# A causal mask in four GpSimd instructions, one per head, in place of one: a memory-augmented attention layer on one Trainium2 core

## The chip, the cores and the metric

The kernel runs on one core of one Trainium2 chip. The metric is the device time of one execution in microseconds (us); smaller is better. Three runs of the kernel before took 332.82, 332.64 and 334.40 us, so its median is 332.82 us.

The core has five engines with queues of their own. In the profile they are PE (TensorE, matrix products; PEld are its weight loads), DVE (VectorE), ACT (ScalarE), POOL (GpSimd) and SP (SyncE, which here only issues DMA transfers). Each works through its own queue in order and waits on semaphores for the others.

## The reference

The input is a sequence of 2048 rows of 640 values in bfloat16. It is normalised, and then goes two ways that are multiplied at the end: a recurrent attention with 32 heads of width 20, and a gated linear unit. The attention goes through the rows in 4 segments of 512. Within a segment each head does causal softmax attention; beside it each head reads a memory that the earlier segments have filled.

```
xn = layernorm(x)
per segment s (512 rows), per head (Dh = 20):
    logits = q k^T * Dh**-0.5 + mask          # mask: key after query -> -1e9
    a_dot  = softmax(logits) v
    a_mem  = (phi(q) M) / (phi(q) z + 1e-6)   # phi(t) = t + 1 if t > 0 else exp(t)
    o      = sigmoid(beta) * a_mem + (1 - sigmoid(beta)) * a_dot
    M += phi(k)^T v ;  z += sum phi(k)
s   = o @ wo
g   = silu( (sigmoid(xn @ w_gate) * (xn @ w_up)) @ w_down )
out = x + s * g
```

## The kernel before

**Tiles.** Rows lie in tiles of 128. The 32 heads are taken in 8 groups of four, and the groups in 4 pairs per segment. The scores of a pair are worked out transposed (keys on the partitions, queries along the free axis), and only the blocks on and below the diagonal. They come in five batches, called units u = 0 to 4 (table `UNITS`, lines 42 to 48). A unit fills one PSUM tile `Sps` of 128 x 4 heads x 512; there is only one such tile, and the function `scores` (line 555) fills it with products of 24 rows, for the four heads side by side on the array. ScalarE then takes the exponential of the whole tile into an SBUF tile `pt` (line 566, four buffers). Units 0 and 3 hold four blocks of the diagonal for each head (unit 0 those of the pair's first group, unit 3 those of its second), and in these the half that the causal mask forbids is set to zero by GpSimd, in place in `pt` (line 569). There are 4 segments x 4 pairs x 5 = 80 units and 32 masks.

**Who uses a masked tile.** `weigh_group` (line 603) multiplies the `pt` tiles of a group with the values into the PSUM tile `AT`, 28 products for four heads, four side by side, with the head as the inner loop; the blocks of unit 0 come first in a first group's products, those of unit 3 last in a second group's, behind 12 others. For the first group of a pair that is at the start of unit 3, three units after its mask; for the second group at the start of the next pair, two units after its mask. ScalarE copies the result to `ats` (line 615), a DMA transposes it (`Asb`, line 618), and VectorE divides by the row sums in `divide`: `rd` (lines 595 and 596) and `od` (line 598). For the last pair `weigh` (line 576) does the same without the detour (`Aps`).

**The rest of the work.** Projections (`v_tile`, `k_chunk`, `q_chunk`), the gated unit (`gate`, `up`, `down`; `hT` at line 484 is its hidden layer on VectorE), the memory (`m_update`, `mem_read`; `om` at line 457), the output projection (`o_proj`, `aa` and `xr` at lines 543 and 549) and the layer norm of the next segment (`ln_stats`, `ln_norm`; `xn` at line 292, transposed by DMA into `xnT`, line 302 or 304) are laid between the units.

**What sets the order.** The program is written out completely by Python. Each unit is a slot; a list of due times by segment (`PLAN`) and the estimated TensorE costs of the tasks say into which slot each task goes. So the order of the instructions in every queue is fixed, and durations on the chip do not change it. On VectorE a late instruction holds up all behind it. The GpSimd queue holds, between the masks: the two steps of `rstd` (lines 280 and 281) that `xn` needs, the additions of `om` to `od` (line 512), those of the memory (line 439), and at the end three of the last additions (line 549). Before the first mask it fills constants with memsets and makes two 0/1 patterns with short affine selects (lines 219 to 251). SP issues all DMAs but the late weights.

Of the kernel before, what the change touches and what calls it, by code (L numbers as in the profile page):

```python
# [9 lines left out]
P = 128  # L10
# [20 lines left out]
ALU = mybir.AluOpType  # L31
# [67 lines left out]
def kernel(  # L99
# [14 lines left out]
    nc = tc.nc  # L114
# [93 lines left out]
    def load_late(name, src, a, b):  # L208
        parts = src.shape[0] // P
        if a == 0:  # L210
# [9 lines left out]
                            base=0, pattern=[[-1, P]], channel_multiplier=1)  # L220
# [86 lines left out]
    def half_tile(tiles, n, half):  # L307
        return tiles[(2 * n + half) % 3]
# [246 lines left out]
    def scores(n, pair, u):  # L555
        half = pair // 2
        qt, kt = half_tile(QT, n, half), half_tile(KT, n, half)
        for (dg, kb, qb, cnt, c0) in UNITS[u]:
            gi = 2 * pair % 4 + dg
            for r in range(4):  # L560
                nc.tensor.matmul(Sps[:, r, c0:c0 + cnt * P],  # L561
                                 lhsT=kt[32 * r:32 * r + KR, gi, kb * P:(kb + 1) * P],
                                 rhs=qt[32 * r:32 * r + KR, gi, qb * P:(qb + cnt) * P],
                                 start=True, stop=True, tile_position=(32 * r, 0))
        pt = ptp.tile([P, 4, L], BF, name="pt")
        nc.scalar.activation(pt[:], Sps[:], ACT.Exp, scale=SCALE)  # L566
        if u in (0, 3):
            diag = pt[:].rearrange("p r (x c) -> p (r x) c", c=P)
            nc.gpsimd.affine_select(out=diag, in_=diag, compare_op=ALU.is_ge, fill=0.0, base=0,  # L569
                                    pattern=[[0, 16], [1, P]], channel_multiplier=-1)  # L570
        return pt

    def parts(dg):
# [193 lines left out]
    for n in range(NSEG):  # L767
# [46 lines left out]
        for slot in range(NSLOT):  # L814
            pair, u = divmod(slot, NU)
            now = NSLOT * n + slot
            share = max(level - fixed[slot], 0.0)
            if u == 0 and (n or pair):
                q = n * (NG // 2) + pair - 1
                weigh_group(now, q // (NG // 2), q % (NG // 2), 1, pts)  # L820
                pts = {}
            elif u == 3 and not old(n, pair):
                weigh_group(now, n, pair, 0, pts)
            pts[u] = scores(n, pair, u)
            delay[0] = True
            goal += FIRST * share
            fill(now + 0.45, (tasks,))
            flush()
            for w in due:
                weigh(*w)  # L830
            delay[0] = False
            while first and first[0][0] < now + 1.0:
                run_task(first)
            due = []
            if old(n, pair) and u in (2, 4):
                due.append((n, pair, u // 4, pts))
            goal += (1.0 - FIRST) * share
            fill(now + 1.0, (tasks, soft))
            split()
# [46 lines left out]
```

## Time and profile before

The profile holds one further execution, of 334.05 us, with a span from first to last instruction of 332.2 us.

| what | value |
|---|---|
| median of three runs | 332.82 us |
| the profiled execution | 334.05 us |
| its span | 332.2 us |
| TensorE clock granted, mean | 0.998 |
| PE busy | 319.7 us |
| DVE busy | 235.4 us |
| ACT busy | 241.6 us |
| POOL busy | 115.6 us, of which 64.5 us are the 32 masks |

In a row of a timeline stand the start in us from the span's start, the duration in us, engine, source line, operation, what is written and read, shapes and count; rows that follow one another on an engine and are alike are merged (x2). A bracket at the end gives the idle time of the engine ahead of it and what ended it. In a row of the waits view stand who waited for whom, the sum in us, how many times, and the longest. Idle time on PE is counted between modelled ends.

### The profile page before, as it was taken

The numbers are of one execution on the slowest core, as the hardware profiler recorded it, in microseconds if no ns is written. First come the engines' busy times: TensorE is split into PE (matmuls) and PEld (weight loads), VectorE is DVE, ScalarE is ACT, GpSimd is POOL, SyncE is SP. The second block draws the span as 40 slices with busy tenths as digits, with TensorE's granted clock in tenths as the row PEclk, the third lists the DMA queues.
The fourth block names the chain that finished last, engine by engine and source line by source line (L and its number), as shares of the span: only waits on it lengthen the run. The fifth ranks groups of instructions, "written<-read, shape, count | busy, mean of one in ns | idle before, by whom it ended". The sixth has DMA issues, their size and how long they took to land.

```text
span 332.2 us, 8456 instructions
## 1 busy us (share of the span) xinstructions
PE 319.7 (96%) x3426; PEld 172.9 (52%) x3426; DVE 235.4 (71%) x516; ACT 241.6 (73%) x271; POOL 115.6 (35%) x137
## 2 busy tenths in 40 slices
PE   8999979999899999999999999999999999899994
PEld 7544445444464564554466455554456555444673
DVE  6276746699779769679976977767666769746545
ACT  3653879898898675686887877776897888688720
POOL 6636222222217022273314522353414232443304
PEclk9999999999999999999999999999999999999999
DMA  7965993598931650444651286134520252320032
GB/s 217 343 215 182 196 210 94 148 217 211 263 106 24 115 128 25 126 126 69 174 137 43 55 136 100 54 108 123 148 78 16 46 128 58 95 77 18 3 63 81
DMA packets 71111, 39.49 MB, mean 119 GB/s; under 512 B 44960, under 2 KB 71072, under 8 KB 71072
## 3 DMA queue, kind: packets, MB, share of 16 engines
q1 hardware_dynamic: 68800, 36.17, 45.1%
q10 hardware_dynamic: 2272, 2.79, 3.1%
q8 instruction: 27, 0.44, 0.5%
q14 instruction: 12, 0.10, 0.1%
HBM read 20.19 MB, written 8.39 MB: 86 GB/s over the span
## 4 chain that ended last, share of the span: by engine, by line
PE 75%; DVE 13%; DMA 7%; issue 3%; ACT 1%; POOL 0%; SPq 0%; DVEq 0%; ACTq 0%
PE yp L499 14%; PE gp L467 13%; PE up L479 12%; PE Sps L561 6%; PE psk L328 6%; PE sp L541 6%; PE AT L611 5%; PE psq L360 5%; PE psv L399 4%; DMA xnT<-xn 4%; DMA Cs<-cb 1%; DVE q L362 1%; PE dm L427 1%; DVE hT L484 1%; DVE rd L596 1%
## 5 line engine op out<-in xcount | busy, mean ns | idle before, releaser
L566 ACT ACTIVATE pt<-Sps 128x2048 bf16<-128x2048 f32 x80 | 150.4, 1880 | 25.4 <-PE Sps L561 25.2
L569 POOL TENSOR_SCALAR_AFFINE_SELECT pt<-pt 128x2048 bf16<-128x2048 bf16 x32 | 64.5, 2017 | 175.3 <-ACT pt L566 175.3
L479 PE MATMUL up<-xnT,Wu 128*128 128x512 bf16 x240 | 63.2, 380 | 0.7 <-DVE aa L543 0.5
L467 PE MATMUL gp<-xnT,Wg 128*128 128x512 bf16 x240 | 62.5, 380 | 0.0
L499 PE MATMUL yp<-Wd,hT 128*128 128x320 bf16 x384 | 56.9, 300 | 1.0 <-DVE hT L484 1.0
L484 DVE SCALAR_TENSOR_TENSOR hT<-tg,up 128x512 bf16<-128x512 bf16 x48 | 32.7, 682 | 18.7 <-PE up L479 13.5
L499 PEld LDWEIGHTS <-hT 128*128 128x128 bf16 x384 | 35.6, 98 | 19.0 <-issue 3.6
L471 ACT ACTIVATE tg<-gp 128x512 bf16<-128x512 f32 x48 | 28.7, 598 | 9.2 <-PE gp L467 9.1
L479 PEld LDWEIGHTS <-Wu 128*128 128x128 bf16 x240 | 21.5, 98 | 25.9 <-issue 4.0
L467 PEld LDWEIGHTS <-Wg 128*128 128x128 bf16 x240 | 21.6, 98 | 24.3 <-issue 2.1
L561 PE MATMUL Sps<-QT,KT 24*128 24x128 bf16 (+2 forms) x896 | 32.5, 241 | 0.8 <-DMA QT<-Cs 0.4
L505 DVE SCALAR_TENSOR_TENSOR aa<-t,yp 128x320 bf16<-128x320 bf16 x32 | 15.3, 481 | 19.3 <-ACT t L503 19.1
L399 PE MATMUL psv<-Wv,xnT 128*128 128x320 bf16 x160 | 25.7, 299 | 2.3 <-DMA xnT<-xn 2.2
L615 ACT CAST ats<-AT 128x512 bf16<-128x512 f32 x30 | 17.6, 586 | 14.0 <-PE AT L611 13.5
L541 PE MATMUL sp<-Wo,oT 128*128 128x320 bf16 x160 | 25.6, 299 | 0.6 <-DVE om L457 0.6
L561 PEld LDWEIGHTS <-KT 24*128 24x128 bf16 x896 | 13.4, 92 | 23.1 <-issue 21.2
L360 PE MATMUL psq<-xnT,Wq 128*128 128x512 bf16 x100 | 23.6, 379 | 0.5 <-DVE q L362 0.5
L328 PE MATMUL psk<-xnT,Wk 128*128 128x512 bf16 x100 | 24.0, 379 | 0.0
L611 PE MATMUL AT<-pt,va 128*32 128x128 bf16 (+1 forms) x840 | 22.1, 244 | 0.8 <-DVE om L457 0.8
L543 DVE SCALAR_TENSOR_TENSOR aa<-aa,sp 128x320 bf16<-128x320 bf16 x32 | 15.4, 483 | 9.1 <-PE sp L541 8.9
L611 PEld LDWEIGHTS <-va 128*32 128x32 bf16 x840 | 14.5, 97 | 13.7 <-issue 6.4
L598 DVE TENSOR_TENSOR od<-Asb,rd 128x320 bf16<-128x320 bf16 x30 | 20.8, 694 | 1.0
(81 smaller groups left out, 374.8 us busy)
## 6 DMA issues: line engine op xcount, KB each, us to landing
KT<-Ks SPq DMA_DIRECT2D x32, 80.0 KB
QT<-Qs SPq DMA_DIRECT2D x32, 80.0 KB
xr<-in_A_x_dram SPq DMA_DIRECT2D x15, 160.0 KB
out_dram<-xr SPq DMA_DIRECT2D x15, 160.0 KB
xt<-in_A_x_dram SPq DMA_DIRECT2D x6, 320.0 KB
Wg<-in_B_w_gate_dram SPq DMA_DIRECT2D x3, 640.0 KB
Wu<-in_B_w_up_dram SPq DMA_DIRECT2D x3, 640.0 KB
Wd<-in_B_w_down_dram ACTq DMA_DIRECT2D x4, 480.0 KB
```

Source lines behind the costliest of these rows:

```text
L328: nc.tensor.matmul(ps[:], lhsT=W["k"][:, k, c * P:(c + 1) * P], rhs=s["xnT"][:, k, :], start=(k == 0), stop=(k == DC - 1))
L360: nc.tensor.matmul(ps[:], lhsT=W["q"][:, k, c * P:(c + 1) * P], rhs=s["xnT"][:, k, :], start=(k == 0), stop=(k == DC - 1))
L399: nc.tensor.matmul(ps[:], lhsT=s["xnT"][:, k, j * P:(j + 1) * P], rhs=W["v"][:, k, half * HB:(half + 1) * HB], start=(k == 0), stop=(k == ...
L467: nc.tensor.matmul(gp[:], lhsT=Wg[f // 4][:, k, fo:fo + P], rhs=s["xnT"][:, k, :], start=(k == 0), stop=(k == DC - 1))
L479: nc.tensor.matmul(ps[:], lhsT=Wu[f // 4][:, k, fo:fo + P], rhs=s["xnT"][:, k, :], start=(k == 0), stop=(k == DC - 1))
L484: empty(lambda: nc.vector.scalar_tensor_tensor(out=h[:], in0=tg[:], scalar=1.0, in1=ps[:], op0=ALU.add, op1=ALU.mult), own)
L499: nc.tensor.matmul(yp[:], lhsT=s["hT"][f][:, j * P:(j + 1) * P], rhs=W["d"][:, f, hs], start=(f == 0), stop=(f == FC - 1))
L541: nc.tensor.matmul(sp[:], lhsT=s["oT"][:, j, c, :], rhs=W["o"][:, c, hs], start=(c == 0), stop=(c == DC - 1))
L561: nc.tensor.matmul(Sps[:, r, c0:c0 + cnt * P], lhsT=kt[32 * r:32 * r + KR, gi, kb * P:(kb + 1) * P], rhs=qt[32 * r:32 * r + KR, gi, qb * P ...
L566: nc.scalar.activation(pt[:], Sps[:], ACT.Exp, scale=SCALE)
L569: nc.gpsimd.affine_select(out=diag, in_=diag, compare_op=ALU.is_ge, fill=0.0, base=0, pattern=[[0, 16], [1, P]], channel_multiplier=-1)
L611: nc.tensor.matmul(AT[32 * r:32 * r + 32, qb * P:(qb + cnt) * P], lhsT=v[:, h0:h0 + 32], rhs=pts[u][:, r, c0:c0 + cnt * P], start=(i == 0) ...
```

## The change

In `scores`, the mask of units 0 and 3 is no longer one affine select over the whole tile (128 partitions x 2048 elements, 16 blocks of 128) but a loop over the four heads. Each of the four instructions handles 128 partitions x 512 elements (4 blocks of 128), in place, with the same condition. Number and place of the calls of `scores` stay as they are; so do all other instructions and their order. In all there are 128 selects in place of 32.

```diff
         nc.scalar.activation(pt[:], Sps[:], ACT.Exp, scale=SCALE)
         if u in (0, 3):
-            diag = pt[:].rearrange("p r (x c) -> p (r x) c", c=P)
-            nc.gpsimd.affine_select(out=diag, in_=diag, compare_op=ALU.is_ge, fill=0.0, base=0,
-                                    pattern=[[0, 16], [1, P]], channel_multiplier=-1)
+            for r in range(4):
+                diag = pt[:, r, :].rearrange("p (x c) -> p x c", c=P)
+                nc.gpsimd.affine_select(out=diag, in_=diag, compare_op=ALU.is_ge, fill=0.0, base=0,
+                                        pattern=[[0, 4], [1, P]], channel_multiplier=-1)
         return pt
```

## The prediction

> **What bounds the kernel now.** I read the page first, then the waits of PE, then the timelines of POOL and DVE side by side. The page:
>
> ```profile
> span 332.2 us, 8456 instructions
> PE 319.7 (96%) x3426; PEld 172.9 (52%) x3426; DVE 235.4 (71%) x516; ACT 241.6 (73%) x271; POOL 115.6 (35%) x137
> ...
> PE 75%; DVE 13%; DMA 7%; issue 3%; ACT 1%; POOL 0%; SPq 0%; DVEq 0%; ACTq 0%
> ...
> L569 POOL TENSOR_SCALAR_AFFINE_SELECT pt<-pt 128x2048 bf16<-128x2048 bf16 x32 | 64.5, 2017 | 175.3 <-ACT pt L566 175.3
> ```
>
> PE is the bound. POOL idles two thirds of the span, a mask takes 2.02 us, and POOL is not on the chain of waits at all. But DVE holds 13% of that chain, some 43 us. So the question is what holds DVE up, and how much of that reaches PE. From the view of the waits, PE's rows that end in DVE, or in a DMA behind DVE:
>
> ```profile
> PE psv L399 <- DMA xnT<-xn: 2.2, 2, 1.8
> PE yp L499 <- DVE hT L484: 1.0, 1, 1.0
> PE AT L611 <- DVE om L457: 0.8, 2, 0.5
> PE sp L541 <- DVE om L457: 0.6, 1, 0.6
> PE up L479 <- DVE aa L543: 0.5, 1, 0.5
> PE psq L360 <- DVE q L362: 0.5, 1, 0.5
> ```
>
> The last five rows sum to 3.4 us, in six waits. The timelines at those places, masks on POOL first, then DVE:
>
> ```profile
> 36.44 2.01 POOL L569 TENSOR_SCALAR_AFFINE_SELECT pt<-pt 128x2048 bf16<-128x2048 bf16 x1 [5.76 <-ACT pt L566]
> ...
> 80.93 2.00 POOL L569 TENSOR_SCALAR_AFFINE_SELECT pt<-pt 128x2048 bf16<-128x2048 bf16 x1 [7.53 <-ACT pt L566]
> ...
> 98.65 2.00 POOL L569 TENSOR_SCALAR_AFFINE_SELECT pt<-pt 128x2048 bf16<-128x2048 bf16 x1 [8.31 <-ACT pt L566]
> ...
> 124.67 2.00 POOL L569 TENSOR_SCALAR_AFFINE_SELECT pt<-pt 128x2048 bf16<-128x2048 bf16 x1 [6.61 <-ACT pt L566]
> ...
> 155.96 2.00 POOL L569 TENSOR_SCALAR_AFFINE_SELECT pt<-pt 128x2048 bf16<-128x2048 bf16 x1 [5.77 <-ACT pt L566]
> ...
> 270.86 2.00 POOL L569 TENSOR_SCALAR_AFFINE_SELECT pt<-pt 128x2048 bf16<-128x2048 bf16 x1 [3.97 <-ACT pt L566]
> ...
> 280.09 2.00 POOL L569 TENSOR_SCALAR_AFFINE_SELECT pt<-pt 128x2048 bf16<-128x2048 bf16 x1 [7.23 <-ACT pt L566]
> ...
> 286.61 2.20 POOL L569 TENSOR_SCALAR_AFFINE_SELECT pt<-pt 128x2048 bf16<-128x2048 bf16 x1 [4.51 <-ACT pt L566]
> 288.78 2.52 POOL L512 TENSOR_TENSOR od<-od,om 128x320 bf16<-128x320 bf16 x3
> ```
>
> ```profile
> 36.36 2.62 DVE L292 TENSOR_SCALAR xn<-xt,mv,rstd 128x640 bf16<-128x640 bf16 x2
> ...
> 81.09 2.19 DVE L598 TENSOR_TENSOR od<-Asb,rd 128x320 bf16<-128x320 bf16 x1
> ...
> 124.93 1.77 DVE L596 TENSOR_TENSOR rd<-rd,omg 128x16 f32<-128x16 f32 x1
> 126.73 0.49 DVE L598 TENSOR_TENSOR od<-Asb,rd 128x320 bf16<-128x320 bf16 x1
> ...
> 156.06 2.25 DVE L598 TENSOR_TENSOR od<-Asb,rd 128x320 bf16<-128x320 bf16 x1
> ...
> 271.91 0.98 DVE L596 TENSOR_TENSOR rd<-rd,omg 128x16 f32<-128x16 f32 x1
> ...
> 280.62 1.82 DVE L549 TENSOR_TENSOR xr<-aa,xr 128x640 bf16<-128x640 bf16 x1
> ...
> 287.15 1.69 DVE L596 TENSOR_TENSOR rd<-rd,omg 128x16 f32<-128x16 f32 x1
> 288.87 1.04 DVE L598 TENSOR_TENSOR od<-Asb,rd 128x320 bf16<-128x320 bf16 x1
> ```
>
> Here is the finding. The same `od` takes 0.49 us at 126.73 and 2.19 us at 81.09. The long one ends at 83.28, 0.35 after the mask that began just ahead of it (80.93 + 2.00 = 82.93); the one at 156.06 ends at 158.31, again 0.35 after its mask. `rd` at 124.93 ends at 126.70 and at 287.15 at 288.84, each 0.03 after its mask's end; `xr` at 280.62 ends 0.35 after. All these read SBUF alone. So such an instruction, caught by a mask, stands until the mask is through, up to 2 us, and DVE's queue stands behind it. Each of PE's six waits above comes behind one of these.
>
> **The change part by part.** First the length of the pieces, and what happens between two of them:
>
> ```profile
> 1.10 0.29 POOL L219 TENSOR_SCALAR_AFFINE_SELECT ident<-ident 128x128 bf16<-128x128 bf16 x1
> ...
> 24.79 0.39 POOL L250 TENSOR_SCALAR_AFFINE_SELECT BD<-BD 128x168 bf16<-128x168 bf16 x1
> 25.13 0.47 POOL L248 TENSOR_SCALAR_AFFINE_SELECT BD<-BD 128x168 bf16<-128x168 bf16 x1
> ```
>
> ```profile
> 24.38 0.97 DVE L292 TENSOR_SCALAR xn<-xt,mv,rstd 128x640 bf16<-128x640 bf16 x2
> ```
>
> Selects of 128 and of 2048 elements take 0.29 and 2.00 us: 0.89 ns an element and 0.18 us fixed, so 0.18 + 512 x 0.89 ns = 0.63 us for a head (bounds: a quarter of 2.00, 0.50, and the 0.39 us of 168 elements plus 344 x 0.89 ns, 0.70). The select at 25.13 begins 0.05 before the end of the one at 24.79 (25.18), whose data it doesn't touch. So four heads take 4 x 0.63 - 3 x 0.05 = 2.37 us, 0.37 more than now (from 4 x 0.50 - 0.15 = 1.85, 0.15 less, to 4 x 0.70 + 3 x 0.07 = 3.0, 1.0 more, with the gap of 0.07 that the dependent select at 24.79 has behind 24.21 + 0.51). Times 32 that is 12 us of POOL, which idles 65%: nothing by itself.
>
> Who waits for the longer mask? PE, at the `AT` products. Where the mask ends nearest to them:
>
> ```profile
> 61.81 0.40 PE L561 MATMUL Sps<-QT,KT 24*128 24x128 bf16 x16
> ...
> 68.84 0.40 PE L561 MATMUL Sps<-QT,KT 24*128 24x128 bf16 x16
> ...
> 101.08 0.81 PE L611 MATMUL AT<-pt,va 128*32 128x256 bf16 x28
> ```
>
> The mask at 98.65 ends at 100.65; the group begins at 101.08, and its masked blocks are the last 16 of 28. So there is at least 0.43 us of cover at the tightest place, and 0.37 fits. On PE itself each head's products now want their own mask: 3 x 32 more waits. At 68.84 the four heads' operands have just come by four separate DMAs, so four waits stand in those 16 products; at 61.81 none do. Both take 0.40 us. I take nothing for a wait already met. The adds and `rstd` behind a mask on POOL come 0.37 us later, at worst once each on the path: I allow 0.4 us in all.
>
> Now the gain. A caught DVE instruction need only wait for the end of one head, if it is let in there. It was at the boundary at 25.18: the second `xn` (the pair ends at 25.35) got through 0.17 after it, while the select of 25.13 was already issued and came out at 0.47 in place of 0.39. The same at 289.57, between two of the three `od` adds of 288.78: the DVE's `od` ends at 289.91. Place by place, with heads ending 0.63, 1.21, 1.79 and 2.37 after the mask's start:
>
> - 81.09 `od`: first head ends 81.56, `od` 81.91 in place of 83.28. 1.4 earlier, PE's 1.0 us goes.
> - 124.93 `rd`: 125.33 in place of 126.70; `od` behind it meets the second head and ends about 126.25 in place of 127.22. 1.0 earlier, the 0.6 goes.
> - 156.06 `od`: 156.94 in place of 158.31; the 0.5 goes.
> - 271.91 `rd`: behind the second head, 272.10; `od` behind the third, 0.4 earlier than now. The first wait of `AT` on `om` (0.3) goes.
> - 280.62 `xr`: 281.07 in place of 282.44; the second (0.5) goes.
> - 287.15 `rd`: 287.47, `od` about 288.4 in place of 289.91; the 0.5 before `up` goes.
>
> That is 3.4 us. The largest of PE's waits is the 1.8 us for `xnT`, behind the two `xn` at 36.36:
>
> ```profile
> 37.24 0.52 SPq L201 DMA_DIRECT2D Wu<-in_B_w_up_dram  x1
> 38.65 5.00 SPq L302 DMA_TRANSPOSE xnT<-xn  x2
> ```
>
> The first `xn` would end at 37.24 in place of 38.62 and the second about 1.1 us sooner; SP is free at 37.76, so the transposes can start 0.9 sooner. Bounds for what arrives: 0 (the transfers in flight set the landing) to 0.9. I take 0.9, because SP's own start is what moves. Sum: 3.4 + 0.9 - 0.4 = 3.9 us. The profiled execution (334.05, span 332.2) would become 330.15; it lay 1.2 above the median, so from the median 332.8 - 3.9 = 328.9 us. Cover of the gain: ahead of PE's next instruction the operands of ACT and DMA must be ready 1 to 4 us sooner than now.
>
> **The rivals.** *Nothing to be measured.* PE runs ahead and meets another wait. For it: ACT is 73% busy, and DMA is behind 2.2 us of PE's waits. Against: those listed ended in DVE, and after 270 us the chain is PE with DVE alone. If only these late ones are kept, 0.3 + 0.5 + 0.5 = 1.3 us: 331.5.
>
> *The heads lock DVE out together; slower.* For it, at the start:
>
> ```profile
> 9.60 0.40 POOL L237 MEMSET nInd<- 128x160 f32 x1
> ```
>
> ```profile
> 9.21 0.98 DVE L292 TENSOR_SCALAR xn<-xt,mv,rstd 128x640 bf16<-128x640 bf16 x1 [0.76 <-POOL rstd L281]
> ```
>
> That `xn` ends 0.18 after the last of a run of memsets, so it was let in between none of them. If four selects queued together do the same, each stall lasts 0.37 longer instead: 6 x 0.37 for PE's six waits, 0.37 for `xnT`, and the 0.4 above, 3.0 us: 335.8. It decides from the point at which the next head holds the ports before the last one has let go. Against: the select at 25.13, which was issued ahead of the other's end and still gave way. The memsets are issued every 0.05 us, many deep; selects of 0.63 us overlap by 0.05. A page speaks for this rival: the Trainium skill, "GPSIMD Engine Reference", section "Instruction dispatch", says that each of the eight cores begins the next instruction as soon as it is done with its own share, with nothing between. By that rule the ports might never be free between heads, and the time would be this rival's 335.8; the memset row agrees with it, the row at 25.13 does not. Another speaks against: the Trainium skill, "SBUF — State Buffer", section "Who interferes with whom", has the GpSimd instruction, or the VectorE instruction with two SBUF inputs or in a two-port mode, hold the shared ports for the whole of that one instruction, whichever issues first. By that rule they come free behind each head, and the time is the forecast's 328.9; the row at 25.13 agrees.
>
> *The heads are dear.* At 1.0 us more per mask (the upper bound) DVE's instructions that slip in push it further, by 0.2 to 0.4 each, and the tightest `AT` waits some 0.7, two or three others less. Some 2 us of the gain is lost: 330.9.
>
> *More than forecast.* More of DVE's instructions are caught than the eight counted; of `od` alone:
>
> ```profile
> L598 DVE TENSOR_TENSOR od<-Asb,rd 128x320 bf16<-128x320 bf16 x30 | 20.8, 694 | 1.0
> ```
>
> At 0.49 apiece 30 would take 14.7 us, so 6.1 us of this is standing still, and the three named hold 4.0 of it. If what the others lose has shortened nothing only because PE's modelled ends hide it (0.2 for each of ten waits), 2 us come on top: 326.9.
>
> **How the numbers follow.** No change is what stays within 0.5%, 1.66 us, about what a measurement of this kernel can tell. The forecast (2.3 to 5 us gained) 0.58, more than that 0.09, dear heads 0.06 (half of it still beyond 0.5%), nothing to be measured 0.14, locked out together 0.13. So faster 0.70, same 0.17, slower 0.13. The likeliest time is 328.9, its own range 327.8 to 330.5. For 8 in 10 I go down to 326.8, to the case of more, and up to 332.5, through most of no change; what is slower is left out.
>
> **What would show it.** In the profile after: 128 selects of about 0.63 us (right between 0.50 and 0.70), four in 2.4 us and up to 0.5 more where DVE slips in. No `rd` over some 0.8, no `od`, `xr` or `xn` over some 1.3 us, and DVE's busy time lower by 10 us or more of 235.4. PE's waits for `hT`, `om`, `aa` and `q` down from 3.4 to below 1 us, the one for `xnT` near 0.9. No new wait of PE for POOL over a few tenths. The `Sps` products stay at 0.40 and `AT` at 0.74 or so. The forecast is wrong if `od` or `rd` still end just after the fourth head (locked out together), if they shorten and PE's waits move to ACT or DMA (the first), or if PE waits for the mask.

## The result, and the profile after

The changed kernel takes 329.24 us (median of 14 runs, 327.56 to 331.30), the kernel before in the same series 333.14 us (14 runs, 331.63 to 334.73). The ratio is 0.988, with a 95% interval of 0.986 to 0.991. The forecast was 328.9 us from a median of 332.8, a gain of 3.9 us; measured is 3.9 (333.14 - 329.24).

The profiled execution took 328.1 us, with a span of 326.2. It lies 1.1 us under its median, and the one profiled before (334.05) 0.9 over its own, so these two differ by 6.0 us, some 2 more than the change gains. From its page the span, the busy times, the chain of waits by engine, and the groups of the new selects and of `od` (both lines have moved by one):

```profile
span 326.2 us, 8552 instructions
...
PE 317.3 (97%) x3426; PEld 172.2 (53%) x3426; DVE 221.9 (68%) x516; ACT 241.4 (74%) x271; POOL 133.2 (41%) x233
...
PE 88%; DMA 7%; DVE 2%; ACT 1%; SPq 1%; issue 0%; POOL 0%; DVEq 0%; ACTq 0%
...
L570 POOL TENSOR_SCALAR_AFFINE_SELECT pt<-pt 128x512 bf16<-128x512 bf16 x128 | 81.8, 674 | 155.4 <-ACT pt L566 155.4
...
L599 DVE TENSOR_TENSOR od<-Asb,rd 128x320 bf16<-128x320 bf16 x30 | 18.8, 628 | 1.0
```

POOL works 17.6 us more, and DVE, with the same instructions, 13.5 us less. DVE's share of the chain went from 13% to 2% (in a second profile of the changed kernel, further down, it is 8%). In the view of the waits, PE's rows are now these:

```profile
PE pT L299 <- DVE xn L292: 1.1, 3, 0.6
...
PE psv L399 <- DMA xnT<-xn: 1.1, 2, 0.9
...
PE up L479 <- DMA Wu<-in_B_w_up_dram: 0.7, 1, 0.7
```

None of the five rows in which PE waited for `hT`, `om`, `aa` or `q` is left. The first row here lies in the first 11 us, ahead of any mask. Two of the places that the prediction worked out, on POOL and then on DVE, with the group whose mask ends closest to it, on PE:

```profile
96.31 2.47 POOL L570 TENSOR_SCALAR_AFFINE_SELECT pt<-pt 128x512 bf16<-128x512 bf16 x4 [7.65 <-ACT pt L566]
...
122.28 2.64 POOL L570 TENSOR_SCALAR_AFFINE_SELECT pt<-pt 128x512 bf16<-128x512 bf16 x4 [6.22 <-ACT pt L566]
...
281.34 2.84 POOL L570 TENSOR_SCALAR_AFFINE_SELECT pt<-pt 128x512 bf16<-128x512 bf16 x4 [3.22 <-ACT pt L566]
```

```profile
122.53 0.41 DVE L597 TENSOR_TENSOR rd<-rd,omg 128x16 f32<-128x16 f32 x1
122.98 0.87 DVE L599 TENSOR_TENSOR od<-Asb,rd 128x320 bf16<-128x320 bf16 x1
...
281.88 0.32 DVE L597 TENSOR_TENSOR rd<-rd,omg 128x16 f32<-128x16 f32 x1
282.23 0.87 DVE L599 TENSOR_TENSOR od<-Asb,rd 128x320 bf16<-128x320 bf16 x1
```

```profile
98.70 0.81 PE L612 MATMUL AT<-pt,va 128*32 128x256 bf16 x28
```

`rd` ends at 122.94, 0.66 us after the mask's start, just behind the first head; `od` ends at 123.85, 1.57 after it, 0.35 behind the second head. The prediction had 0.66 and 1.58 there. POOL pays: with `od` in between, four heads take 2.64 and 2.84 us instead of 2.4. The mask of 96.31 ends at 98.78, 0.08 into the group that begins at 98.70; its products on masked blocks are the last 16, and nothing waits.

Where the time went is seen by cutting the span at one point of the chain, the 15 products that wait for the DMA of the second segment's `xnT`. Before, and then after:

```profile
47.12 2.21 PE psv L399 x15
```

```profile
46.12 2.21 PE psv L399 x15
```

Ahead of it the two executions differ by 1.0 us, behind it by (332.2 - 47.12) - (326.2 - 46.12) = 285.1 - 280.1 = 5.0. Of the 1.0 us, 0.8 is there already when the first mask begins (at 36.44 and at 35.64), so the change did not make it. The 5.0 belong to these two executions; a second profile of the changed kernel, in the experiments below, takes 281.6 us behind the point, which is 3.5 less than before.

### The profile page after: what moved, and what is told of

The parts are those of the page before. It is cut to its first block, busy times and chain, and to the rows that moved or that the text cites. A ratio compares the mean times of both kernels' runs of the same rounds, so it can differ in the third digit from the quotient of the medians.

```text
span 326.2 us, 8552 instructions
## 1 busy us (share of the span) xinstructions
PE 317.3 (97%) x3426; PEld 172.2 (53%) x3426; DVE 221.9 (68%) x516; ACT 241.4 (74%) x271; POOL 133.2 (41%) x233
## 4 chain that ended last, share of the span: by engine, by line
PE 88%; DMA 7%; DVE 2%; ACT 1%; SPq 1%; issue 0%; POOL 0%; DVEq 0%; ACTq 0%
PE gp L467 16%; PE up L479 15%; PE yp L499 15%; PE Sps L561 8%; PE psk L328 7%; PE sp L541 7%; PE psq L360 6%; PE AT L612 6%; PE psv L399 5%; DMA xnT<-xn 4%; DMA xt<-in_A_x_dram 1%; PE am L449 1%; DMA Qs<-q 1%; PE dm L427 1%; PE Aps L584 1%; ACT pt L566 1%
## 5 line engine op out<-in xcount | busy, mean ns | idle before, releaser
L570 POOL TENSOR_SCALAR_AFFINE_SELECT pt<-pt 128x512 bf16<-128x512 bf16 x128 | 81.8, 674 | 155.4 <-ACT pt L566 155.4
L616 ACT CAST ats<-AT 128x512 bf16<-128x512 f32 x30 | 17.6, 586 | 11.8 <-PE AT L612 11.1
L599 DVE TENSOR_TENSOR od<-Asb,rd 128x320 bf16<-128x320 bf16 x30 | 18.8, 628 | 1.0
```

## The experiments

The theory: a DVE instruction that needs the ports which GpSimd's reading uses stands until the end of the one select that caught it; shorter selects let it in sooner, and PE behind it. The rivals: PE gains because the first heads are masked sooner; or the mask's end, or POOL's busy time, is what counts. Ratios are to the kernel before on the same chip; the edits are shown against the changed kernel, and `...` stands for lines left out.

**Two selects per mask.**

```diff
-            for r in range(4):
-                diag = pt[:, r, :].rearrange("p (x c) -> p x c", c=P)
+            for r in (0, 2):
+                diag = pt[:, r:r + 2, :].rearrange("p r (x c) -> p (r x) c", c=P)
...
-                                        pattern=[[0, 4], [1, P]], channel_multiplier=-1)
+                                        pattern=[[0, 8], [1, P]], channel_multiplier=-1)
```

> Two selects per mask, each of two heads (128 x 1024), in place of four. Theory (a caught DVE instruction stands until the end of the one GpSimd instruction that caught it): pieces of about 1.1 us, so the longest `rd` near 1.2 us, between the 1.77 of one piece and the 0.67 of four; DVE busy between 235 and 222 us, near 227; the time gains half to two thirds of what four pieces gain, 1.7 to 2.7 us, ratio 0.992 to 0.995. Rival (PE begins sooner because the first heads are masked sooner): about half the gain too, so this run alone does not tell the two apart, but then DVE's busy time has no reason to lie between.

Measured: 330.58 us, ratio 0.993 (0.990 to 0.996), DVE busy 228.2 us. A select takes 1.12 us, and the longest `rd` 1.04 us. The groups of `od` and `rd`, of two selects:

```profile
L599 DVE TENSOR_TENSOR od<-Asb,rd 128x320 bf16<-128x320 bf16 x30 | 20.0, 666 | 1.0
...
L597 DVE TENSOR_TENSOR rd<-rd,omg 128x16 f32<-128x16 f32 x32 | 10.2, 320 | 1.1
```

`od` at 666 ns lies between 694 of one piece and 628 of four. The gain is as the theory said, 0.7% of the 1.2%; the two intervals just touch.

**Four selects by columns.** Equally many and equally long, but each over all heads, so that no head is done before the last.

```diff
-            for r in range(4):
-                diag = pt[:, r, :].rearrange("p (x c) -> p x c", c=P)
+            for x in range(4):
+                diag = pt[:, :, x * P:(x + 1) * P]
```

> Four selects per mask, each of one block column of 128 for all four heads, so the same lengths as one per head, but no head is finished before the fourth select. Theory (the ports come free between selects): as with one per head, ratio 0.985 to 0.991, DVE busy 220 to 224 us. Rival (the first heads being ready sooner is what counts): no gain, ratio 0.998 to 1.003, with DVE busy unchanged against the changed kernel or not.

Measured: 328.82 us, ratio 0.988 (0.983 to 0.993), DVE busy 222.3 us. The whole gain is there, so it isn't that the first heads are ready sooner. That rival is out. One of the six waits stays in this profile: the first one of `AT` for `om` is 0.5 us.

**Eight selects.**

```diff
             for r in range(4):
-                diag = pt[:, r, :].rearrange("p (x c) -> p x c", c=P)
+                for y in (0, 2):
+                    diag = pt[:, r, y * P:(y + 2) * P].rearrange("p (x c) -> p x c", c=P)
...
-                                        pattern=[[0, 4], [1, P]], channel_multiplier=-1)
+                                            pattern=[[0, 2], [1, P]], channel_multiplier=-1)
```

> Eight selects per mask, half a head each (128 x 256, about 0.41 us; a mask takes some 2.9 us). Theory: DVE is let in more often, its busy time falls a little more, to 218 to 221 us, but the mask ends 0.5 us later, and where PE's products follow it by 0.3 to 0.5 us with four pieces (three places) PE now waits for POOL, up to 0.3 us each. Ratio 0.986 to 0.991, no clear difference from four. Rival (what counts is the mask's end): slower than four by the 0.5 us at each tight place and by what it hands on, ratio 0.990 to 0.995.

Measured: 330.44 us, ratio 0.992 (0.989 to 0.996); DVE busy 217.5 us, less than with four. The ratio is just outside what I expected and inside what I gave for the rival (what counts is the mask's end); its interval meets that of four pieces, so this run alone decides nothing between the two. The mask of 98.29 in this run takes 3.42 us, and PE, for the first time, stands for POOL:

```profile
101.40 0.63 PE L613 MATMUL AT<-pt,va 128*32 128x128 bf16 x13 [0.17 <-POOL pt L571]
```

That is 0.2 us in all and does not make up a loss of 1 us. In this profile the first mask already begins 1.2 us later than with four pieces (36.81 against 35.64), and behind the cut it takes 329.3 - 47.70 = 281.6 us. The rest of the loss, if there is one, is open.

**No mask.**

```diff
         if u in (0, 3):
-            for r in range(4):
...
+            pass
```

> The causal mask is left out altogether (all else stays), so no GpSimd instruction of this line holds the ports. It is the ceiling of the theory: the 10 us or so by which DVE instructions are still stretched with four pieces go, DVE busy near 212 us. PE's waits behind DVE were already gone with four pieces, so the time falls only a little below it: 326.5 to 329 us where the kernel before takes 333, ratio 0.981 to 0.988. If it is clearly below 0.980, more of the time hung on the masks than the six waits and `xnT`.

Measured: 327.16 us, ratio 0.983 (0.979 to 0.988), DVE busy 210.4 us. Beside four pieces by columns in the same series (328.82) that is 1.7 us less, with intervals that overlap. PE's wait for `xnT`, and the same point of the chain as above:

```profile
PE psv L399 <- DMA xnT<-xn: 1.9, 2, 1.6
```

```profile
46.36 2.21 PE psv L399 x15
```

Two things follow. Behind the point the kernel without any mask takes 326.4 - 46.36 = 280.0 us; four pieces took 280.1 in the profile above and 281.6 in the second one, so between nothing and 1.6 us is left to gain there. And the wait of 1.6 us for `xnT` stands although no select holds `xn`.

**A memset in place of the mask.** About as long as the whole select, but it only writes.

```diff
-            for r in range(4):
-                diag = pt[:, r, :].rearrange("p (x c) -> p x c", c=P)
-                nc.gpsimd.affine_select(out=diag, in_=diag, compare_op=ALU.is_ge, fill=0.0, base=0,
-                                        pattern=[[0, 4], [1, P]], channel_multiplier=-1)
+            nc.gpsimd.memset(pt[:], 1.0)
```

> In place of the mask each diagonal batch gets one memset of the whole `pt` tile to 1.0 (so the scores of these batches are lost and the mask too): about 1.8 us of GpSimd at the same place, which writes SBUF and reads nothing. If what locks is the reading (the shared read port), instructions with two SBUF inputs (`rd`, `od`, `xr`) stay at 0.18, 0.49 and 0.49 us under it, while `xn`, `aq` and `q` + 1, with one input, may still be caught; DVE busy 210 to 220 us, ratio 0.982 to 0.992. If every long GpSimd instruction locks, whatever it does, `rd` and `od` are stretched to 1.5 us and more as with the whole mask, DVE busy is 230 us or more and the ratio 0.995 to 1.0.

Measured: 328.29 us, ratio 0.984 (0.980 to 0.987), DVE busy 219.1 us. Groups by line, of this run:

```profile
L568 POOL MEMSET pt<- 128x2048 bf16 x32 | 57.8, 1806 | 176.5 <-ACT pt L566 176.5
...
L596 DVE TENSOR_TENSOR od<-Asb,rd 128x320 bf16<-128x320 bf16 x30 | 15.2, 507 | 1.0
...
L292 DVE TENSOR_SCALAR xn<-xt,mv,rstd 128x640 bf16<-128x640 bf16 x16 | 11.2, 708 | 0.8 <-POOL rstd L281 0.8
...
L363 DVE TENSOR_SCALAR aq<-q 128x512 uint16<-128x512 uint16 x20 | 8.6, 432 | 1.9 <-ACT q L362 1.3
```

The same groups with no mask at all:

```profile
L596 DVE TENSOR_TENSOR od<-Asb,rd 128x320 bf16<-128x320 bf16 x30 | 14.8, 492 | 1.0
...
L292 DVE TENSOR_SCALAR xn<-xt,mv,rstd 128x640 bf16<-128x640 bf16 x16 | 7.6, 478 | 2.3 <-DMA xnT<-xn 1.5 <-POOL rstd L281 0.8
...
L363 DVE TENSOR_SCALAR aq<-q 128x512 uint16<-128x512 uint16 x20 | 5.8, 288 | 1.9 <-ACT q L362 1.3
```

A GpSimd instruction of 1.8 us that reads nothing leaves `od`, with two inputs from SBUF, at 507 against 492 ns. `xn` and `aq`, with one, are caught all the same: 708 against 478, 432 against 288. So it isn't POOL's being busy alone that stops DVE; it matters what the two instructions read and write. The Trainium skill, page "SBUF — State Buffer", section "Who interferes with whom", has just this: two SBUF inputs contend with a GpSimd instruction that reads SBUF and not with one that only writes it, and the two-port modes, which `tensor_scalar` can enter, contend with both. The trace agrees in both halves: `od` takes 694 ns beside whole selects and 507 beside memsets, `xn` 748 and 708. That it is the ports is the page's account; what the runs show is that it goes by the kind of the two instructions.

**The mask of unit 0 twice, whole.** The second changes nothing in the data.

```diff
-            for r in range(4):
-                diag = pt[:, r, :].rearrange("p (x c) -> p x c", c=P)
+            diag = pt[:].rearrange("p r (x c) -> p (r x) c", c=P)
+            for again in range(2 if u == 0 else 1):
...
-                                        pattern=[[0, 4], [1, P]], channel_multiplier=-1)
+                                        pattern=[[0, 16], [1, P]], channel_multiplier=-1)
```

> One select per mask as before, but the mask of unit 0 is done twice (the second changes nothing): 16 selects of 2.0 us more, 32 us more of POOL busy, each as long as before; PE's products follow this mask by 2.9 us and more. Theory (what counts is how long one instruction stands, and each further one catches again): more catches of up to 2 us, DVE busy 245 to 255 us, slower, ratio 1.005 to 1.02. Rival (only POOL's share of time or the mask's end counts): no change here while the cover of 2.9 us holds, ratio 0.997 to 1.003.

Measured: 338.38 us, ratio 1.014 (1.011 to 1.018), DVE busy 250.4, POOL 150.8 us. PE's waits:

```profile
PE Sps L561 <- ACT pt L566: 1.9, 1, 1.9
...
PE psq L360 <- DVE q L362: 1.4, 2, 0.8
PE up L479 <- DVE hT L484: 1.3, 2, 1.0
...
PE AT L612 <- DVE om L457: 1.2, 2, 0.6
...
PE yp L499 <- DVE hT L484: 1.0, 1, 1.0
```

With 0.6 us of `sp` behind `om` and 0.5 of `gp` behind `aa`, PE's waits behind DVE in the masks' part of the span come to 6.0 us, where the kernel before had 3.4. Why `Sps` waits 1.9 us for ScalarE was not tried.

**The mask of unit 0 twice, by heads.**

```diff
-            for r in range(4):
-                diag = pt[:, r, :].rearrange("p (x c) -> p x c", c=P)
+            for again in range(2 if u == 0 else 1):
+                for r in range(4):
+                    diag = pt[:, r, :].rearrange("p (x c) -> p x c", c=P)
...
```

> Four selects per mask, and the mask of unit 0 is done twice, eight selects of 0.63 us (the second four change nothing): POOL busy about as with two whole selects, some 170 us, but in short pieces. Theory: near the changed kernel, ratio 0.986 to 0.994, DVE busy 223 to 230 us. If POOL's busy time were what costs, it would be as slow as two whole selects.

Measured: 332.88 us, ratio 0.995 (0.992 to 0.999), DVE busy 230.0, POOL 176.6 us. This separates the two plainly: POOL works 61 us more than in the kernel before (115.6), 26 us more than with two whole selects, and the kernel is a little faster than the one and clearly faster than the other. Doubling the mask is not free for all that: beside four pieces done once (ratio 0.988) it costs 0.7%, and the ratio lies just above what I expected. Its waits show where:

```profile
PE psv L399 <- DMA xnT<-xn: 3.7, 3, 1.7
```

and on POOL one sees what it may come from:

```profile
181.88 5.16 POOL L571 TENSOR_SCALAR_AFFINE_SELECT pt<-pt 128x512 bf16<-128x512 bf16 x8
187.02 0.45 POOL L280 TENSOR_SCALAR rstd<-mv 128x1 f32<-128x1 f32 x1
```

The last `rstd` of the next segment, which `xn` needs, stands behind eight selects. That this is what made `xnT` late was not tried by itself.

**Four pieces in the last segment only.**

```diff
-            for r in range(4):
-                diag = pt[:, r, :].rearrange("p (x c) -> p x c", c=P)
+            for r in range(4 if n == NSEG - 1 else 1):
+                diag = (pt[:, r, :].rearrange("p (x c) -> p x c", c=P) if n == NSEG - 1
+                        else pt[:].rearrange("p r (x c) -> p (r x) c", c=P))
...
-                                        pattern=[[0, 4], [1, P]], channel_multiplier=-1)
+                                        pattern=[[0, 4 if n == NSEG - 1 else 16], [1, P]], channel_multiplier=-1)
```

> Four selects per mask in the last segment only (8 of 32 masks), one in the others. By the forecast's list three of PE's waits go, those in front of `AT` twice and of `up`, 1.3 us as idle time between modelled ends, up to 1.8 us by the spacing of the starts; the waits at 83, 127 and 158 us stay. Ratio 0.993 to 0.997. If the gain were spread over all masks alike, a quarter of it, ratio 0.997.

Measured: 332.98 us, ratio 0.998 (0.996 to 1.001). The waits that should go are gone but for 0.2 of the first, and the three in the earlier segments stand where they did:

```profile
PE yp L499 <- DVE hT L484: 1.0, 1, 1.0
...
PE sp L541 <- DVE om L457: 0.6, 1, 0.6
PE psq L360 <- DVE q L362: 0.5, 1, 0.5
...
PE AT L613 <- DVE om L457: 0.2, 1, 0.2
```

```profile
45.31 2.21 PE psv L399 x15
```

Behind the cut this is 328.7 - 45.31 = 283.4 us, 1.7 less than the 285.1 of before, as expected. The runs do not bear it out: the ratio lies above the range that I gave, the gain is 0.5 us with an interval from 1.5 gained to 0.5 lost, and the profiled execution (331.02) is the fastest of its twelve. In these runs differences of 1 us are at the edge of what can be seen. The first mask is whole here, and yet the cut comes at 45.31, sooner than in any profile shown so far.

**Four pieces again, and eight in unit 0 with four in unit 3.** The first edit is the change itself, the second:

```diff
-            for r in range(4):
-                diag = pt[:, r, :].rearrange("p (x c) -> p x c", c=P)
+            step = 2 if u == 0 else 4
+            for r in range(4):
+                for y in range(0, 4, step):
+                    diag = pt[:, r, y * P:(y + step) * P].rearrange("p (x c) -> p x c", c=P)
...
```

> The changed kernel again, beside the next one on the same chip: ratio 0.986 to 0.991.

> Eight selects of half a head in unit 0, whose products come 2.9 us and more behind the mask with four pieces, and four selects of a head in unit 3, whose products come as close as 0.3 us. Theory: the cost of eight pieces in unit 3 (PE and ScalarE waiting for POOL) goes, and DVE's busy time is near 219 us. As four pieces already leave no wait of PE behind DVE, the time is that of four pieces, within 0.003 of the ratio measured beside it. If DVE's busy time itself counted, it would be faster by 0.003 or more.

Measured: 329.60 and 329.50 us, both with ratio 0.988 (0.983 to 0.993, 0.984 to 0.992). DVE is busy 221.7 and 219.1 us; the 2.6 us less are worth nothing that these runs can show. No version that still masks is clearly faster than four pieces.

The changed kernel has a second profile here, of an execution of 330.27 us with a span of 328.5. Its point of the chain, and one of the six waits, which is still there:

```profile
46.92 2.21 PE psv L399 x15
```

```profile
PE AT L612 <- DVE om L457: 0.3, 1, 0.3
```

Behind the cut it takes 328.5 - 46.92 = 281.6 us, 1.5 more than the first profile of the same kernel. Of that, 0.3 is this wait and 0.7 one for an `xnT` at 201.67, neither of which the first profile has. So a single profile tells such differences to some 1.5 us only. From one select to two and to four the time from the cut to the end falls all the same, and with eight no further: 285.1 us for one, 282.4 for two, 280.1, 281.6 and (by columns) 281.3 for four, 281.6 for eight, 280.0 without a mask.

## Why the prediction was right, and where it was not

The mechanism was right; the size of the sum to a tenth of a microsecond is luck, as the terms below show.

**The finding** that DVE's long instructions are stretched by the mask, and not by their own work, held: with no mask `od` takes 492 ns on average and `xn` 478, and DVE's busy time falls by 25 us. With four pieces the longest `rd` takes 0.67 us (1.77 before) and the longest `od` 1.03 (2.33 before). **That DVE is let in between two heads** held as well, to 0.01 us at the first of the two places shown. So "locked out together" is out. **The length of a head**: 0.63 us forecast, 674 ns on average (median 634), the longer ones presumably where DVE holds POOL up; four in 2.4 us, and up to 0.4 more where `od` slips in. "The heads are dear" is out: no wait of PE for POOL appears, and the `AT` group closest to its mask takes 0.81 us as before.

**The six waits of PE**, 3.4 us: all gone in the first profile, and all but the first one of `AT` (0.3, and 0.5 by columns) in the two others with four pieces, so that term held but for these tenths. By the cut the gain behind the point is 5.0 us in the first profile and 3.5 in the second. How the excess of the first comes about is argued only. A part may be in how idle time is counted: between modelled ends. In the chain before, five products in a row take 1.09 us, 0.22 each, while the page counts each at 379 ns:

```profile
86.97 1.09 PE psq L360 x5
```

So up to 0.16 us of each wait may hide under the end of the product in front, by estimate 1.0 us for six waits. That was in the prediction only as the rival "more than forecast". A second wait for `xnT`, of 0.4 us (2.2 less 1.8), near 204 us went too in that execution; in the second profile it is there with 0.7 us, at 201.67, so it differs between executions of one kernel.

**The 0.9 us for `xnT`** is the step that failed. The rule I gave, that SP's own start is what moves, was only the next limit in line. The chain from that start to the landing, before, with four pieces, and in the second profile of four pieces:

```profile
38.65 8.42 DMA xnT<-xn
```

```profile
37.02 9.05 DMA xnT<-xn
```

```profile
38.21 8.67 DMA xnT<-xn
```

Counted from the start of the first mask, SP starts 2.2 us behind it before, 1.4 and 2.0 us with four pieces: in the first profile that is 0.8 sooner, as forecast. But the landing then takes 0.6 us longer, and the cut comes 10.5 us after the start of the first mask (46.12 - 35.64) where it was 10.7 (47.12 - 36.44): 0.2 and not 0.9. In the second profile it is 10.7 again (46.92 - 36.22). That is the lower bound that the prediction named and did not take, that the transfers in flight set the landing; it fits that the DMA engines' share is 0.99 or more in every microsecond from 37 to 45, before and in the first profile after, but it was not tried by itself.

With four pieces DVE's second `xn` has a new wait as well:

```profile
35.55 0.91 DVE L292 TENSOR_SCALAR xn<-xt,mv,rstd 128x640 bf16<-128x640 bf16 x1
37.51 0.79 DVE L292 TENSOR_SCALAR xn<-xt,mv,rstd 128x640 bf16<-128x640 bf16 x1 [1.05 <-DMA xnT<-xn]
```

The row names an earlier transpose, which presumably still reads the buffer that `xn` is to write. It does not seem to set the landing: this `xn` ends at 38.30, and SP, busy with the first transpose, comes to the second only at 40.6.

PE's wait at the cut did go from 1.8 to 0.9 us, the value forecast, and that is luck: 0.2 of it is the earlier landing, the other 0.7 is PE itself, which gets there later, behind waits of 0.7 us for `Wu` (0.2 before) and 0.2 for another `xnT`. The wait is 1.6 us with no mask at all and 0.9 with the first mask whole. From the start of the first mask to the cut it takes 10.0 to 10.7 us in the three profiles with that mask whole (once done twice), and 9.5 to 10.7 in the three with four pieces, so the landing doesn't go by the mask.

**The 0.4 us of allowance** for what stands behind a mask on POOL did not show as a wait of PE; with masks twice as long (eight selects) it may have. So the sum came out for errors that offset one another: 0.7 to 0.9 too much for `xnT`, against 0.4 of allowance that did not show and up to 1.0, by estimate, for the hidden part of the six waits. How the measured 3.9 us divides is not known more closely than that.

**The rivals.** "Nothing to be measured" is out by the runs: the interval of the ratio ends at 0.991. That ACT or DMA would take up the gain is seen at a few places only (PE for `Wu` 0.7 us where it was 0.2).

## What to carry to other kernels

An instruction that is off the chain by itself may sit on it through another engine's instruction that it holds up. Look on VectorE for instructions of one kind that take several times as long at some places as at others, and see whether they end just behind the end of a GpSimd instruction: then cutting the GpSimd instruction into pieces lets them in, even though GpSimd works longer. Stop cutting where the wait of the bound engine is gone: eight pieces brought nothing here that four had not, and they make the GpSimd result later (3.42 us for the mask at 98.29).

## What was not expected of the hardware

A memset of 1.8 us on GpSimd leaves `od`, with two SBUF inputs, nearly untouched (507 ns against 492) but stretches `xn` with one (708 against 478); I had asked the question, but not known that one run would show both sides of it. And the kernel with the masks of unit 0 done twice is 5.5 us faster by heads (332.88) than with whole selects (338.38), although by heads GpSimd is busy 26 us longer.
